# Products with v moved into the transposes' PSUM ring, with a new planner clock and new ranks

## The chip, the cores and the metric

The kernel runs on one core of one Trainium2 chip. What counts is device time in microseconds (us), from an execution's start to its end; with one core there is no slowest core to look for.

## What is computed

The reference runs three layers, one after another, in float32: attention that keeps only the 32 largest scores of each row, a dense layer with the gate h * cos(h), and a routed layer in which eight experts take 288 tokens each, handed out in the order of the logits.

```python
scores = scale * np.matmul(q, k.transpose(0, 1, 3, 2))          # 4 batches, 8 heads, 576 x 576, depth 64
kth = np.partition(scores, -top_k, axis=-1)[..., -top_k:-top_k + 1]
scores = np.where(scores >= kth, scores, -1000000000.0)
attn = np.exp(scores - np.max(scores, axis=-1, keepdims=True))
attn = attn / (np.sum(attn, axis=-1, keepdims=True) + 1e-09)
x = np.matmul(attn, v)                                          # then (2304, 512)
h = x @ w_in; y = (h * np.cos(h)) @ w_out                       # 512 -> 2048 -> 512
h = np.maximum(y[mask] @ w1[e], 0.0); out[mask] = h @ w2[e]     # per expert e, 288 tokens each
```

## The kernel before

**Stages.** The program has three stages. The first (phase1) runs attention and, behind it, the dense layer, interleaved. The second, the tail, finishes the dense layer and decides which token goes to which expert. The third runs the experts. The change touches the first stage and the ranks of the second.

**Attention in units.** Attention is cut into 72 units of 128 query rows with two "halves" h. The first eight (NWR) hold the 64 query rows left over from each head; the other 64 hold 128 rows of two heads each, and two units in a row share keys, queries and v (a pair, one `key`). Eight of these whole units feed one block of 256 tokens of the dense layer. One unit goes through these steps:

- qk (L555): PE (TensorE) writes half of the scores into the PSUM tile `two`, two banks; evac (L562): ACT (ScalarE) copies them into the tile x. This is done twice per unit, and both halves use the same columns of `two`, so the second qk follows the first evac.
- topk: DVE (VectorE) takes element-wise maxima and minima of the two halves (L596, L602) and then finds the 32 largest values by rounds of MAX8 and MATCH_REPLACE8 (L605, L609, L612); ACT, POOL (GpSimd) and DVE mask, exponentiate (L640) and clear (L645).
- tr (L710): PE transposes x into a PSUM tile of the ring pT, which has two tiles; eT (L720): ACT copies it out. Three such pieces belong to a whole unit.
- pv (L735, L737): PE multiplies eT with v. The result lies in `two` as well, in the columns behind the scores, one place per pair.
- The row sums become factors: div (L770, POOL), recip (L765, DVE), wide (L774, POOL), Rm (L781, PE, a transpose into the ring pT), Re (L784, ACT, into R), all once per pair; then scale (L798, DVE) multiplies pv's result of both units with R into xr. For the first eight units, scale is L795 and the factors are made per unit.

**The dense layer.** Each block's xr is split into a high and a low part xH, xL (L848, L853). mm1 (L287) makes hidden columns in pieces of 12 matmuls; sine and gate follow on ACT, DVE and POOL (`less` is L318 on DVE); mm2 (L887) multiplies back into the PSUM tiles pY in pieces of six. Of the eight banks of PSUM, `two`, pT, the hidden tiles pH and pY take two each.

**What sets the order.** A planner (class Plan) does. Each step is a task with an engine, a cost in ns, tasks it comes after, ring tiles it takes and gives back, and a rank: the unit or block number plus an offset per kind of task from the table OFFSETS (kinds of the first eight units end in _r, of the first block in _0). The planner simulates the engines, starts the earliest startable task of the lowest rank, and emits the instructions in that order; on the chip, each engine's queue runs strictly in it. For PE it adds a cost SW where the array's mode changes between tasks (scores 64x128, pv 128x64, the rest 128x128) and HOLD_PE to the rank of a task in another mode. The tail has a plan of its own, with TAIL_OFFSETS.

**Rings in pT.** Transposes of x, of the weights (wt), of y (yt), the small logit products and Rm take a tile of pT in the order of the plan, in turn; a tile is taken again when its reader has finished.

Of the kernel before, what the change touches and what calls it, by code (L numbers as in the profile page):

```python
# [14 lines left out]
AF = mybir.ActivationFunctionType  # L15
# [11 lines left out]
def f32(ap):  # L27
# [11 lines left out]
    "L": 4, "Re": 0.25, "Re_0": -5.25, "Re_r": 4.5, "Rm": 3.5, "Rm_0": -7.5, "Rm_r": -4.5, "bias": 7.25, "bias_0":  # L39
    2.75, "bias_r": -2, "big": -3, "big_0": -2.75, "big_r": -5.75, "count": -2, "div": 8, "div_0": 1.25, "div_r":  # L40
# [3 lines left out]
    -3.25, "large": 7.5, "large_0": 1, "large_r": 5.5, "less": 2.25, "less_0": 4.75, "low_in": -4.25, "low_out": 4,  # L44
# [3 lines left out]
    -5.5, "scale": -3.5, "scale_0": -1, "scale_r": -1.5, "sg_in": -10, "sg_out": 7, "shift_in": -9.75, "shift_out":  # L48
    -5.5, "sine": -4.5, "sine_0": 4, "small": 2.5, "small_0": -3.75, "small_r": -7.5, "strike": 3.75, "strike_0": 8,
    "strike_r": 6.25, "top": 7.25, "top_0": 7.25, "top_r": -3, "total": -8, "tr": -4, "tr_0": -10, "tr_r": -1.75,  # L50
    "v": 7.5, "wH_in": 6.25, "wH_out": -9.5, "wL_in": -3.25, "wL_out": -6.5, "w_in": 7, "w_out": 9.75, "whole": -5,
    "wide": -6, "wide_0": -5.25, "wl": 4, "wl_0": 3.25, "wp": 2.5, "wraw_in": 6.75, "wraw_out": -3.25, "wse": -1.75,
    "wst_out": -5.75, "wt": -9, "wte": -0.5, "xH": -5.75, "xL": -0.5, "yT": -10, "yd": -6.25, "ys": 4.75, "yt":
    0.75, "zero": 0.5, "zero_0": -5, "zero_r": -5.25
# [5 lines left out]
    "L": 3.75, "all": 0.75, "am": -3.5, "amd": -4.25, "any": -4.75, "asg": 0, "before": 0.75, "cmp": -4.75, "cnt":  # L60
    8.25, "columns": -9, "excess": -4, "first": 6.25, "gH": -6.75, "gH_e": -10, "gL": 5, "gL_e": -1.5, "gate": 1.25,
    "here": 1.75, "higher": -1.75, "hs": 1.75, "in_column": 0.5, "in_row": 1, "less": -8.5, "lg": -7, "lg4": 0.5,
    "listed": -1, "lt": 1.5, "mm1": 1.5, "mmT": 0.75, "near": -0.25, "next": -6.75, "numbers": 5.25, "places": 2.25,
    "prop": -3.75, "rise": -5.5, "rows": -3.5, "shares": 4, "sine": -3, "slots": -8, "square": -7.5, "start": 3.25,
    "sums": -5.5, "tokens": 0.25, "verdict": -2.5, "wh": 1.5, "wl": 6, "wlo": 7, "woL": 1, "woL_e": 0.75, "wrong":
    -10, "y": -1.5, "y_e": 3.25, "yd": 5, "yd_e": -0.5, "ys": -8, "ys_e": -6.75
# [3 lines left out]
class Plan:  # L70
# [6 lines left out]
    SW = 200  # L77
    HOLD_PE = 1.5
# [18 lines left out]

    def run(self):
        ts = self.tasks
        users, giver, left = {}, {}, {}  # L100
# [26 lines left out]
        while len(order) < len(ts):  # L127
# [54 lines left out]
def fused_kernel(ctx: ExitStack, tc: tile.TileContext, qT: bass.AP, kT: bass.AP, qR: bass.AP, kR: bass.AP, v9: bass.AP,  # L182
# [5 lines left out]
    HP = H // 2  # L188
# [54 lines left out]
    def everything(fold, ctx):  # L243
# [134 lines left out]
        def phase1():  # L378
# [13 lines left out]
            for vt in vts:  # L392
# [4 lines left out]
                pS=1, pPV=1, pT=2, pH=2, pY=1,  # L397
# [141 lines left out]
            def qk(j):  # L539
# [1089 lines left out]
```

## Time and profile before

| | |
|---|---|
| median of 3 runs | 1176.52 us (1175.04 to 1177.78) |
| profiled execution, its own time | 1176.04 us |
| its span, first to last instruction | 1174.1 us |
| PE busy | 1031.8 us (88%) |
| DVE busy | 903.1 us (77%) |
| ACT busy | 796.9 us (68%) |
| POOL busy | 515.2 us (44%) |
| mean granted clock of PE | 0.958 |

The profile is of one execution; 1.9 us of its time lie around the span. A row of the views below names engine, line and tiles: `PE two L555` is the scores' matmul of line 555 into the tile `two`. "A <- B" under waits means that A's engine stood idle until B was done. A busy time counts a matmul from its start to the end of its last result, so that matmuls in a row overlap: their steps are read from their starts.

### The profile page before, as it was taken

What the parts mean: (1) busy time and instruction counts of PE and PEld (TensorE: products, weight loads), DVE (VectorE), ACT (ScalarE), POOL (GpSimd) and SP (SyncE); (2) the same over time, 40 slices, a digit from 0 to 9 for tenths busy, and PEclk for the clock granted to TensorE, in tenths of its full rate; (3) what the DMA queues carried; (4) which work ended last, traced back from release to release, by engine and by line L of the source; (5) the groups of instructions that cost most, each with busy time, mean ns of one, the idle gap of its engine ahead of it and who ended that gap; (6) DMA issues with size and microseconds to landing.
All of it is one profiled execution on the core that took longest, in us unless ns stands there. A gap on an engine that the chain in (4) does not pass through costs nothing.

```text
span 1174.1 us, 22307 instructions
## 1 busy us (share of the span) xinstructions
PE 1031.8 (88%) x7952; PEld 861.6 (73%) x7952; DVE 903.1 (77%) x2443; ACT 796.9 (68%) x1431; POOL 515.2 (44%) x645
## 2 busy tenths in 40 slices
PE   4676898999899999999999999998898599999995
PEld 1344776777677777777777777777776499999995
DVE  6989999998898888888888888886469365555530
ACT  5876798888788787787887886888341255555531
POOL 5865676666554454454454553544200202222211
PEclk9876998999999999999999999999899899999998
DMA  7564353443323323223323223210043776666611
GB/s 228 164 184 150 108 158 113 129 148 115 104 89 98 94 78 100 85 82 97 92 81 103 80 82 102 79 55 6 34 160 128 228 211 201 185 187 198 185 40 43
DMA packets 86029, 141.08 MB, mean 120 GB/s; under 512 B 15248, under 2 KB 36240, under 8 KB 85904
## 3 DMA queue, kind: packets, MB, share of 16 engines
q1 hardware_dynamic: 82832, 130.07, 36.0%
q0 software_dynamic: 3072, 9.44, 2.7%
q8 instruction: 66, 1.08, 0.4%
q14 instruction: 59, 0.48, 0.1%
HBM read 125.85 MB, written 13.63 MB: 119 GB/s over the span
## 4 chain that ended last, share of the span: by engine, by line
PE 50%; issue 16%; ACT 14%; DVE 12%; POOL 5%; DMA 2%; SPq 0%; POOLq 0%; ACTq 0%; DVEq 0%
PE pH L287 13%; PE pY L887 11%; PE two L555 7%; PE two L737 4%; PE pT L710 4%; ACT x L562 4%; DVE w L609 2%; DVE m L605 2%; POOL out L1539 2%; PE pY L1403 2%; ACT eT L720 1%; PE ph L1507 1%; PE po L1522 1%; DVE cmp L1168 1%; PE two L735 1%
## 5 line engine op out<-in xcount | busy, mean ns | idle before, releaser
L605 DVE MAX8 m<-w 128x8 f32<-128x288 f32 (+1 forms) x576 | 238.1, 449 | 0.9
L555 PE MATMUL two<-kp,qp 64*128 64x288 f32 (+1 forms) x640 | 130.2, 496 | 77.6 <-ACT x L562 62.4
L609 DVE MATCH_REPLACE8 w<-m,w 128x288 f32<-128x288 f32 x432 | 188.8, 443 | 0.0
L287 PE MATMUL pH<-xH,wiH 128*128 128x256 f32 x576 | 173.7, 302 | 1.0 <-DVE kr L318 0.6
L287 PE MATMUL pH<-xL,wiH 128*128 128x256 f32 x576 | 163.8, 284 | 0.9 <-POOL xL L853 0.9
L287 PE MATMUL pH<-xH,wiL 128*128 128x256 f32 x576 | 163.4, 284 | 0.0
L562 ACT ACTIVATE x<-two 128x576 f32<-128x576 f32 x144 | 93.1, 646 | 71.6 <-PE two L735 56.3
L555 PEld LDWEIGHTS two<-kp,qp 64*128 64x128 f32 (+1 forms) x640 | 49.8, 189 | 123.6 <-ACT x L562 89.6
L720 ACT ACTIVATE eT<-pT 128x384 f32<-128x384 f32 x224 | 106.5, 480 | 23.1 <-PE pT L710 18.0
L633 POOL TENSOR_TENSOR x<-x,w 128x576 f32<-128x576 f32 x76 | 107.3, 1424 | 20.4 <-ACT w L627 20.2
L287 PEld LDWEIGHTS pH<-xH,wiH 128*128 128x128 f32 x576 | 110.3, 191 | 7.9 <-issue 5.6
L287 PEld LDWEIGHTS pH<-xL,wiH 128*128 128x128 f32 x576 | 110.8, 192 | 1.6 <-POOL xL L853 1.3
L287 PEld LDWEIGHTS pH<-xH,wiL 128*128 128x128 f32 x576 | 110.5, 192 | 0.0
L1023 DVE TENSOR_TENSOR w2l<-w2raw,w2h 128x1024 fp32r<-128x1024 f32 x64 | 77.9, 1223 | 41.8 <-ACT w2h L1020 41.8
L710 PE MATMUL pT<-ident,x 128*128 128x128 f32 x576 | 98.3, 280 | 2.2 <-ACT wog L830 1.5
L1539 POOL DMA_INDIRECT out<-ot,idx x24 | 22.3, 928 | 177.3 <-ACT ot L1537 176.9
L887 PE MATMUL pY<-wo,gH 128*128 128x512 f32 x224 | 95.5, 426 | 0.0
L710 PEld LDWEIGHTS pT<-ident,x 128*128 128x128 f32 x576 | 68.0, 141 | 31.7 <-issue 15.5
L328 POOL TENSOR_TENSOR hs<-hs,kr 128x512 f32<-128x512 f32 x56 | 73.1, 1312 | 40.6 <-ACT kr L323 34.2
L872 POOL TENSOR_TENSOR gL<-hs,gH 128x512 fp32r<-128x512 f32 x56 | 74.7, 1334 | 35.2 <-ACT gH L868 17.7
L887 PE MATMUL pY<-wl,gH 128*128 128x512 f32 x224 | 89.1, 398 | 0.0
L887 PE MATMUL pY<-wo,gL 128*128 128x512 f32 x224 | 88.2, 394 | 0.0
(220 smaller groups left out, 2874.8 us busy)
## 6 DMA issues: line engine op xcount, KB each, us to landing
w2raw<-w SPq DMA_DIRECT2D x64, 512.0 KB, 3.7
wl<-wl_d SPq DMA_DIRECT2D x112, 256.0 KB, 2.6
vt<-v SPq DMA_DIRECT2D x48, 256.0 KB, 2.7
kp<-kT SPq DMA_DIRECT2D x32, 288.0 KB, 3.2
room<-w_in SPq DMA_DIRECT2D x16, 512.0 KB, 5.0
room<-w_out SPq DMA_DIRECT2D x16, 512.0 KB, 3.5
woL<-wl_d SPq DMA_DIRECT2D x16, 512.0 KB, 3.6
kp<-kR SPq DMA_DIRECT2D x16, 288.0 KB, 4.3
```

Of the source, the lines that this page charges most:

```text
L287: PE.matmul(ph, lw[:, c, fs], rx[:, c, :], start=(k == 0), stop=(k == 3 * KD - 1))
L328: (G if m - 1 + i in GATE_POOL else V).tensor_tensor(h, h, T["kr", m // 2][:, 2 * i:2 * i + 2], op=OP.mult)
L555: PE.matmul(o, lhsT, T["kp", us[h]][p, s], start=True, stop=True)
L562: A.activation(T["x", j][:, :, c * hS:(c + 1) * hS], T["pS", (j, c)][:, :, :hS], AF.Copy)
L605: V.max(m8_(h, 8 * k), w_(h, 0, hS + (8 if k == TOPK // 8 - 1 else 0)) if fold else w_(h))
L609: V.match_replace(w, m8_(h, 8 * k), x_(h) if k == 0 and not fold else w, -BIG)
L633: G.tensor_tensor(x_(h), x_(h), w_(h), op=OP.subtract if mode == "S" else OP.add)
L710: PE.transpose(pT[:, i, :], e[:, c0:c0 + 128], ident)
L720: A.activation(new(ap, "eT", (j, c), [128, 3, 128])[:, :n], T["pT", ("e", j, c)][:, :n], AF.Copy)
L872: (G if m in GL_POOL else V).tensor_tensor(gL, T["hs", m], f32(T["gH", m]), op=OP.subtract)
L887: PE.matmul(T["pY", blk][t], T[g, m][:, i, ts], w, start=(f == 0 and n == 0), stop=(f == KF - 1 and n == 2))
L1023: eng.tensor_tensor(WS[n][1], WR.pop(n), f32(WS[n][0]), op=OP.subtract)
```

## The change

Three things change together.

**The products with v get a tile of the ring pT, one per unit.** pv takes a ring tile and no longer writes `two`. All that follows is done unit by unit instead of pair by pair: div, recip, wide, Rm, Re and scale run 64 times in place of 32 for the whole units, each on half the columns; the eight leftover units keep their count. pv now comes after Rm of its own unit, and the second piece of transposes of a unit comes after the pv of the unit before (the first piece, in the leftover units).

**The planner's costs.** The cost of a change of mode falls from 200 to 95 ns, HOLD_PE from 1.5 to 0; qk from 690 to 590 and pv from 1260 to 985. PE's work is now charged by a function that follows how busy the planned PE has been and counts its work at half speed while it takes the clock to be halved.

**The ranks** in OFFSETS and TAIL_OFFSETS are all replaced, so the order changes everywhere in the first stage, and a little in the second. Two lines of that table stand for it here.

```diff
-    "L": 4, "Re": 0.25, "Re_0": -5.25, "Re_r": 4.5, "Rm": 3.5, "Rm_0": -7.5, "Rm_r": -4.5, "bias": 7.25, "bias_0":
+    "L": -3.75, "Re": -2.25, "Re_0": -5.5, "Re_r": 6, "Rm": 4, "Rm_0": -2.25, "Rm_r": 5.5, "bias": 7, "bias_0":
...
-    SW = 200
-    HOLD_PE = 1.5
+    SW = 95
+    HOLD_PE = 0
...
+    def clock(self):
+        act, slow, since, W = 0.0, False, 0, self.WINDOW
+        def work(s, w):
...
+                speed = 0.5 if slow else 1.0
...
+        return work
...
+        work = self.clock()
...
-            f = s + t["ns"] + (self.TABLE if sw else 0)
             if t["mode"]:
-                f += self.SW if t["mode"] != mode else 0
+                f = work(s, t["ns"] + (self.SW if t["mode"] != mode else 0))
                 mode = t["mode"]
+            else:
+                f = s + t["ns"] + (self.TABLE if sw else 0)
...
-                pS=1, pPV=1, pT=2, pH=2, pY=1,
+                pS=1, pT=2, pH=2, pY=1,
...
                 def prod():
-                    if rem or t % 2 == 0:
-                        T["pPV", u] = two[:, :, hS:hS + 128]
-                    o_ = T["pPV", u]
+                    o_ = new(psum, "pT", ("pv", j), [128, 128])
...
-                    if c == 0 and ("Rm", key(j - 2, 0)) in plan.tasks and closes(j - 2):
-                        last.append(("Rm", key(j - 2, 0)))
+                    if j and c == (0 if rem else 1):
+                        last.append(("pv", j - 1))
...
-                add(("pv", j), "PE", 1700 if rem else 1260, prod, need + ([("pv", j - 1)] if j else []),
-                    [("pPV", u)] if rem or t % 2 == 0 else [],
+                add(("pv", j), "PE", 1700 if rem else 985, prod, need + [("Rm", j)] + ([("pv", j - 1)] if j else []), [("pT", "pv", j)],
                     need[:len(chunks)] + [("vt", w) for w in ((u, u + 1) if rem else (u, ))], rank=rank)
-                if not close:
-                    return
...
-                    G.tensor_scalar(ri[:, :, c], rs[:, :, c], TWO_PI, TWO_PI * 1e-9, op0=OP.mult, op1=OP.add)
+                    G.tensor_scalar(new(ap, "ri", j, [128, 2]), T["rs", j], TWO_PI, TWO_PI * 1e-9, op0=OP.mult, op1=OP.add)
...
-                        V.tensor_mul(xr[:, hp].rearrange("p (t q) -> p t q", t=2), pv_, R)
+                        V.tensor_mul(xr[:, hp, t % 2 * 128:(t % 2 + 1) * 128], o_, R[:, 0])
...
-                add(("scale", j), "DVE", 620 if rem else 345, scale, [("Re", u), ("pv", j)], [("xr", blk)] if firstw else [],
-                    [("R", u), ("pPV", u)], rank=rank)
+                add(("scale", j), "DVE", 620 if rem else 200, scale, [("Re", j), ("pv", j)], [("xr", blk)] if firstw else [],
+                    [("R", j), ("pT", "pv", j)], rank=rank)
```

Three places show how the order moves. Numbers behind a name tell buffers apart; line numbers of the change are its own (L589 is qk, L742 tr, L767 and L769 pv, L802 Rm, L325 mm1).

**Places 1 and 2, on PE, middle of the first stage.** Before: a unit's second qk, the products of an earlier unit, the next unit's first qk.

```order
L710 MATMUL pT_6689<-ident_64,x_6409 128x128 x3
L555 MATMUL two_119<-kp_6204,qp_6181 128x288 x2
L737 MATMUL two_119<-eT_6631,vt0_120 64x128 x3
L737 MATMUL two_119<-eT_6653,vt0_120 64x128 x3
L737 MATMUL two_119<-eT_6700,vt0_120 64x128 x2
L735 MATMUL two_119<-eT_6700,vt0_120 64x128 x2
L555 MATMUL two_119<-kp_6466,qp_6436 128x288 x2
L710 MATMUL pT_6732<-ident_64,x_6409 128x128 x3
```

The products stand between two qk there. Of the change, the same step, and as place 2 the two rows behind it:

```order
L589 MATMUL two_119<-kp_5955,qp_5896 128x288 x2
L769 MATMUL pT_6395<-eT_6319,vt0_120 64x128 x3
L769 MATMUL pT_6395<-eT_6347,vt0_120 64x128 x3
L769 MATMUL pT_6395<-eT_6382,vt0_120 64x128 x2
L767 MATMUL pT_6395<-eT_6382,vt0_120 64x128 x2
L589 MATMUL two_119<-kp_6171,qp_6146 128x288 x2
L742 MATMUL pT_6418<-ident_64,x_6121 128x128 x3
L802 MATMUL pT_6422<-ident_64,rw_6386 128x128
```

What stands side by side is the same, but the products write pT_6395, a ring tile, and not `two`. Behind them a piece of transposes takes the other tile of the ring, and Rm (pT_6422) the one that pT_6395 held; between the products and that Rm stand one qk and one tr.

On DVE, the scaling that gives such a tile back stood once per pair in the rounds of the top-k search, 128x256 long (xr is the scaled result, R the factors):

```order
L609 MATCH_REPLACE w_6439<-m8_6440,w_6439 128x288 x2
L605 MAX m8_6440<-w_6439 128x8 x2
L609 MATCH_REPLACE w_6439<-m8_6440,w_6439 128x288 x2
L605 MAX m8_6440<-w_6439 128x8 x2
L798 TENSOR_TENSOR xr_5782<-two_119,R_6565 128x256
L596 TENSOR_TENSOR w_6602<-x_6533 128x2x288
L645 SCALAR_TENSOR_TENSOR x_6409,rs_6548<-x_6409,m8_6440,w_6439 128x576
L602 TENSOR_TENSOR w_6602<-x_6533 128x2x288
```

It reads `two`, which qk writes. Now it stands there once per unit, 128x128:

```order
L643 MATCH_REPLACE w_6285<-m8_6286,w_6285 128x288
L639 MAX m8_6286<-w_6285 128x8 x2
L356 TENSOR_TENSOR kr_6202<-pH_6211,kr_6202 128x512
L643 MATCH_REPLACE w_6285<-m8_6286,w_6285 128x288 x2
L820 TENSOR_TENSOR xr_5901<-pT_6395,R_6349 128x128
L630 TENSOR_TENSOR w_6415<-x_6375 128x2x288
L639 MAX m8_6286<-w_6285 128x8
L636 TENSOR_TENSOR w_6415<-x_6375 128x2x288
```

It reads the ring tile pT_6395 of place 2, and stands ahead of the next unit's first top-k step (L630).

**Place 3, on PE, from the first stage to the tail.** Before, the last products were followed by the logit products L355, which read the table wog_, and only then by mm1 of the last block.

```order
L710 MATMUL pT_9547<-ident_64,x_9233 128x128 x3
L737 MATMUL two_119<-eT_9537,vt1_121 64x128 x3
L737 MATMUL two_119<-eT_9551,vt1_121 64x128 x3
L737 MATMUL two_119<-eT_9554,vt1_121 64x128 x2
L735 MATMUL two_119<-eT_9554,vt1_121 64x128 x2
L355 MATMUL pp_9647<-room_104,wog__9620 32x256 x16
L287 MATMUL pH_9678<-xH_101,wiH_99 128x256
L287 MATMUL pH_9678<-xL_102,wiH_99 128x256
L287 MATMUL pH_9678<-xH_101,wiL_100 128x256
```

Behind L355 stood all of that mm1. In the change:

```order
L742 MATMUL pT_9935<-ident_64,x_9629 128x128 x3
L802 MATMUL pT_9940<-ident_64,rw_9912 128x128
L769 MATMUL pT_9947<-eT_9930,vt1_121 64x128 x3
L769 MATMUL pT_9947<-eT_9933,vt1_121 64x128 x3
L769 MATMUL pT_9947<-eT_9942,vt1_121 64x128 x2
L767 MATMUL pT_9947<-eT_9942,vt1_121 64x128 x2
L325 MATMUL pH_10039<-xH_101,wiH_99 128x256
L325 MATMUL pH_10039<-xL_102,wiH_99 128x256
L325 MATMUL pH_10039<-xH_101,wiL_100 128x256
```

Now mm1 of the last block follows at once; four pieces of it, 48 matmuls, stand ahead of the logit products (L393 in the change).

## Rows read from the trace of the kernel before

**Rows 1.** Busy us (xinstructions) of PE, PEld, DVE, ACT, POOL; granted clock, DMA share, GB/s
```profile
0.00:118.90 118.90, 73.54 (x572) 40.87 (x572) 100.15 (x291) 79.60 (x155) 79.22 (x84) 0.81 0.59 182
118.90:226.70 107.80, 94.86 (x702) 77.09 (x701) 100.57 (x270) 91.89 (x173) 75.60 (x84) 0.92 0.41 127
226.70:818.10 591.40, 547.34 (x4276) 446.26 (x4275) 515.31 (x1531) 478.64 (x860) 296.73 (x388) 1.00 0.30 89
```

**Rows 2.** The same view for one period of the long stretch
```profile
572.68:659.13 86.45, 79.76 (x618) 64.78 (x617) 74.80 (x225) 68.77 (x123) 42.16 (x57) 1.00 0.30 89
```

**Rows 3.** Waits of PE, 226.7 to 818.1: us in total, times, longest us
```profile
PE two L555 <- ACT x L562: 39.0, 51, 0.8
```

**Rows 4.** Timeline of PE: start us, us, line, out<-in, [idle before <-releaser]
```profile
514.08 0.76 PE L555 MATMUL two<-kp,qp 64*128 64x288 f32 x4
514.76 1.09 PE L737 MATMUL two<-eT,vt 128*64 128x128 f32 x16
515.69 0.39 PE L735 MATMUL two<-eT,vt 128*64 128x128 f32 x4
516.85 0.76 PE L555 MATMUL two<-kp,qp 64*128 64x288 f32 x4 [0.78 <-ACT x L562]
```

**Rows 5.** Timeline of ACT, same place
```profile
516.15 0.65 ACT L562 ACTIVATE x<-two 128x576 f32<-128x576 f32 x1 [1.61 <-PE two L735]
```

**Rows 6.** Waits of DVE, 226.7 to 818.1
```profile
DVE w L596 <- ACT x L562: 24.8, 17, 4.0
DVE xr L798 <- PE two L555: 22.8, 12, 3.4
```

**Rows 7.** Timeline of PE, hidden matmuls and the scores behind them
```profile
500.65 0.28 PE L287 MATMUL pH<-xL,wiH 128*128 128x256 f32 x1
500.77 0.28 PE L287 MATMUL pH<-xH,wiL 128*128 128x256 f32 x1
500.99 0.76 PE L555 MATMUL two<-kp,qp 64*128 64x288 f32 x4
```

**Rows 8.** Groups of 226.7 to 818.1: shapes xcount | busy us, mean ns | idle before
```profile
L798 DVE TENSOR_TENSOR xr<-two,R 128x256 f32<-128x256 f32 x27 | 11.3, 420 | 23.4 <-PE two L555 22.8 <-ACT R L784 0.3
L765 DVE RECIPROCAL ri<-ri 128x4 f32<-128x4 f32 x28 | 4.5, 162 | 0.3 <-POOL ri L770 0.3
L770 POOL TENSOR_SCALAR ri<-rs 128x4 f32<-128x4 f32 x28 | 10.3, 369 | 78.7 <-DVE x L645 73.3 <-DVE fa L964 4.7
L774 POOL COPY rw<-ri 128x256 f32<-128x256 f32 x28 | 11.6, 416 | 10.0 <-DVE ri L765 10.0
```

**Rows 9.** Groups of 0 to 118.9, DVE
```profile
L795 DVE TENSOR_TENSOR xr<-two,R 64x128 f32<-64x128 f32 x14 | 4.0, 288 | 2.8 <-PE two L555 2.4
```

**Rows 10.** Waits of DVE, 0 to 118.9
```profile
DVE room L435 <- ACT room L428: 8.8, 2, 6.1
DVE w L596 <- ACT x L562: 2.6, 2, 2.3
DVE xr L795 <- PE two L555: 2.4, 1, 2.4
```

**Rows 11.** Waits of DVE, 118.9 to 226.7
```profile
DVE xr L798 <- PE two L555: 3.1, 3, 1.6
DVE xr L795 <- PE two L555: 1.7, 1, 1.7
```

**Rows 12.** Waits of PE, 0 to 118.9
```profile
PE two L555 <- DVE xr L795: 5.8, 3, 3.3
```

**Rows 13.** Timeline of PE, end of the attention phase
```profile
817.67 0.44 PE L735 MATMUL two<-eT,vt 128*64 128x128 f32 x4
826.50 3.64 PE L355 MATMUL pp<-room,wog__9620 128*32 128x256 f32 x32 [8.40 <-DVE wog__9620 L1077]
```

**Rows 14.** Timeline of DVE, same place
```profile
820.39 0.42 DVE L853 TENSOR_TENSOR xL<-xr,xH 128x256 fp32r<-128x256 f32 x1
825.58 0.56 DVE L1077 COPY wog__9620<-wog 128x128 f32<-128x128 f32 x1
```

More of the change, by code (lines that the diff above doesn't have):

```diff
@@ L50 @@
[L50 to L54, printed above, removed]
+    "L": -3.75, "Re": -2.25, "Re_0": -5.5, "Re_r": 6, "Rm": 4, "Rm_0": -2.25, "Rm_r": 5.5, "bias": 7, "bias_0":
@@ L59 @@
 TAIL_OFFSETS = {
[L60 to L66, printed above, removed]
+    "L": 5.25, "all": -6.25, "am": -7.5, "amd": 5, "any": -0.5, "asg": 6.75, "before": -5, "cmp": -8, "cnt": -1.75,
+    "columns": 2.75, "excess": -5.75, "first": 1.5, "gH": 1.5, "gH_e": 1, "gL": 5, "gL_e": 0.5, "gate": -3.5,
+    "here": 1.5, "higher": 2.25, "hs": -3.25, "in_column": -1.75, "in_row": 4, "less": 3.25, "lg": -4.75, "lg4":
+    -1.5, "listed": -7, "lt": -1.25, "mm1": -2.25, "mmT": 4.25, "near": 5, "next": 2.5, "numbers": 7.75, "places":
+    2, "prop": -7, "rise": -0.75, "rows": 6.25, "shares": -0.75, "sine": 0.25, "slots": -6, "square": -1.5, "start":
+    -5.5, "sums": 6, "tokens": -0.5, "verdict": 3.5, "wh": -7, "wl": -7.75, "wlo": -4.75, "woL": -8.5, "woL_e": -6,
+    "wrong": -7, "y": 0.75, "y_e": 1.75, "yd": 3.75, "yd_e": 1.25, "ys": 0.75, "ys_e": 4.75
 }
@@ L783, in spread_out @@
+                    for n in range(2 if rem else 1):
+                        PE.transpose(p[:, n], T["ri", j][:, n:n + 1].to_broadcast([128, 128]) if rem else
+                                     T["rw", j].rearrange("p h d -> p (h d)"), ident)
                 def spread_out():
-                    A.activation(new(ap, "R", u, [128, 2, 128]), T["pT", ("R", u)], AF.Copy)
+                    A.activation(new(ap, "R", j, [128, 2, 128])[:, :2 if rem else 1], T["pT", ("R", j)], AF.Copy)
                 blk = 0 if rem else 1 + (j - NWR) // (2 * HP)
@@ L808, in pv @@
-                firstw = j == 0 if rem else (j - NWR) % (2 * HP) == 1
-                add(("scale", j), "DVE", 620 if rem else 345, scale, [("Re", u), ("pv", j)], [("xr", blk)] if firstw else [],
-                    [("R", u), ("pPV", u)], rank=rank)
+                        V.tensor_mul(xr[:, hp, t % 2 * 128:(t % 2 + 1) * 128], o_, R[:, 0])
+                exps = [("zero" if MODES[j] == "T" else "exp", a) for a in range(2 * j, 2 * j + 2)]
+                add(("div", j), "POOL", 190, div, exps, [("ri", j)], [("rs", j)], rank=rank)
@@ new lines, in pv @@
+                add(("recip", j), "DVE", 85, recip, [("div", j)], rank=rank)
+                if not rem:
+                    add(("wide", j), "POOL", 300, wide, [("recip", j)], [("rw", j)], [("ri", j)], rank=rank)
+                add(("Rm", j), "PE", 220 if rem else 110, spread, [("recip" if rem else "wide", j)], [("pT", "R", j)],
+                    [("ri" if rem else "rw", j)], rank=rank)
+                add(("Re", j), "ACT", 265 if rem else 165, spread_out, [("Rm", j)], [("R", j)], [("pT", "R", j)], rank=rank)
@@ L856, in block @@
                 for c in range(HP):
-                    need = [("scale", w) for w in last if unit(w)[2] // 2 == c // 2] if blk == 0 else [("scale", last[c])]
+                    need = [("scale", w) for w in last if unit(w)[2] // 2 == c // 2] if blk == 0 else [("scale", last[2 * c + i]) for i in range(2)]
                     add(("xH", blk, c), *(("DVE", 340) if (blk, c) == LAST else ("ACT", 310)), x_high(c), need + ([("xH", blk, c - 1)] if c else []),
```

91 lines of the change are left out of this document (54 added, 37 removed), and 9 rows, old and new, of the table OFFSETS.

## Prediction, written before the changed kernel was run

> **What bounds the kernel now.** I read the table of stretches first, since the share of busy time over the whole span mixes four stages. Up to 226.7 us VectorE (DVE) is the fuller engine: 100.15 of 118.9 us, then 100.57 of 107.8, against 73.54 and 94.86 for TensorE (PE) [rows 1]. From 226.7 to 818.1 us PE takes over: 547.34 of 591.4 us at a granted clock of 1.00 (the 2.4 GHz level), DVE 515.31. In that stretch the work repeats: eight units of attention and eight hidden pieces every 86.45 us, with PE busy 79.76 and DVE 74.80 [rows 2]. A microsecond that PE saves there is a microsecond of the kernel, as long as DVE can follow.
>
> Next the waits. PE's 44 us of idleness in the stretch are nearly one item: 51 times scores (L555) waited for the evacuation of the scores before (ScalarE, ACT, L562), 39.0 us, at most 0.8 each [rows 3]. The timeline shows why. Scores start at 514.08; the products with v (L737, L735) follow and end at 515.69 + 0.39 = 516.08; the next scores start at 516.85, after 0.78 us of waiting [rows 4]. The evacuation of the first scores, ready to run at 514.84, starts at 516.15, just after the last product [rows 5]: scores and products lie in the same two PSUM banks, and the read is held until PE has stopped writing there. The same sharing hits DVE: its scaling of the products (L798) waited 22.8 us for PE's scores, and its first top-k step (L596) 24.8 us for the evacuation [rows 6].
>
> **The change part by part.** *Products out of `two`.* The evacuation (0.65 us) now runs beside the products, which take 514.76 to 516.08 = 1.32 us: it is done before PE has finished them, so the 39.0 us go. Place 1 shows scores, products, scores still side by side; they need not move.
>
> *More changes of array mode.* Scores, products and the rest each have a mode of the array. By the order, PE changes mode 32 times per eight units before, 36 after. Hidden matmuls start 0.12 us apart (500.65, 500.77), the scores behind them 0.22 after the last [rows 7]: a change costs 0.10 us. The stretch is 591.4 / 86.45 = 6.8 periods, so 4 x 6.8 = 27 more, +2.7 us. The Trainium skill (TensorEngine Tiling (Array Packing), Key Properties) says that a change of tiling mode drains TensorE, which speaks against the new order; were a whole matmul's 0.28 us exposed at each change, not the step's 0.12, a change would be an estimated 0.16 and the sum 1.6 us later. The row shows less, and I stay with it.
>
> PE's floor of the stretch: 591.4 - 39.0 + 2.7 = **555.1 us**.
>
> *Scaling per unit on DVE.* 27 scalings of 128x256 at 420 ns become 54 of 128x128 [rows 8]. No row has that shape: half of 420 is the lower end (0 more in all), 420 unchanged the upper (+11.3). I take 288, that of the 64x128 scaling [rows 9], nearest in columns: 54 x 0.288 - 27 x 0.420 = +4.2. The reciprocals double, 28 x 0.162 = +4.5. DVE work: 524.0 us. DVE is idle for 591.4 - 515.3 = 76.1 us; without the 22.8 (the false wait for scores) and the 24.8 there are 28.5 left. So DVE's path is 524.0 + 28.5 = 552.5 us if the waits for the evacuation vanish, 577.3 if all stay, 564.9 with half. Each evacuation comes up to 1.3 us earlier, 17 x 1.3 = 22 of the 24.8; but only where nothing else is late.
>
> Floor (555.1) and DVE (552.5 to 564.9) thus lie on top of each other, and two full engines in step lose a little to each other. I take the middle of 555.1 and 564.9, **560.0: -31.4 us**. Ends: 577.3 (-14.1), and 547.3 + 2.7 = 550.0 if PE's other waits vanish too (-41.4).
>
> *Cost at nothing.* POOL gets 28 more divisors and 28 more widenings, 28 x (0.369 + 0.416) = 22.0 us [rows 8], on 296.7 busy in 560: hidden behind PE and DVE. ACT gets 27 copies of R, at most an evacuation's 0.65 each, 17.6 on 478.6: 496 of 560, hidden; were ACT the bound, those 17.6 would be the price. PE transposes as many R columns as before.
>
> *The new wait.* The products now need R's transposes first, so divisor, reciprocal and widening (0.369 + 0.162 + 0.416 = 0.95 us and three hand-overs) stand ahead of them. Place 2 has that transpose behind the first three transposes of x; queued behind it on PE are mm2 and the next products, and ACT and DVE wait for those. This is why I take the middle, not the floor.
>
> *The start (0 to 226.7).* DVE sets it. False waits of the same kind are 2.6 + 2.4 [rows 10] and 3.1 + 1.7 us [rows 11], 9.8 together; five pairs add 5 x (0.576 - 0.420 + 0.162) = 1.6. Half of 9.8 less 1.6: **-3.3**. The ranks are new here, so ends far apart: all DVE idleness but the 8.8 for the first weights gone, 26.0 - 8.8 - 1.6 = -15.6; or +5.8, if PE's wait for scalings there (5.8) [rows 12] comes back at the ring.
>
> *The hand-over.* After the last products, at 817.67 + 0.44 = 818.11, PE waits until 826.50 for a table that DVE finishes at 825.58 + 0.56 = 826.14 [rows 13, 14]. Place 3: 48 hidden matmuls (48 x 0.12 = 5.8 us) now come first; they need xL, ready at 820.39 + 0.42 = 820.81. They fill 826.50 - 820.81 = **-5.7**; other end 0, if the last hidden pieces aren't what the routing waits for. Behind it the rows of the order stay the same.
>
> Sum: -31.4 - 3.3 - 5.7 = -40.4 on the profiled execution's 1176.04: 1135.6. Its time is 0.48 under the median of the runs, so I forecast **1136 us**. Ends: -41.4 - 15.6 - 5.7 = -62.7 (1114) and -14.1 + 5.8 + 0 = -8.3 (1168).
>
> **The rivals.**
>
> *The ring stalls (slower).* A product holds one of two ring tiles until DVE has scaled it; in place 2 the second request behind it (R's transpose) comes 0.68 (scores) + 3 x 0.12 = 1.04 us after the products. If DVE is behind by the mean of today's waits between the two, 22.8 / 12 = 1.9 us, PE waits 1.9 + 0.29 - 1.04 = 1.15 us in each of 64 units, 73 us: **1209**. It decides from 40.4 / 64 = 0.63 us per unit. For it: in the start, where DVE is the bound, PE did wait for scalings [rows 12]. Against it: in the long stretch DVE waits for PE, not PE for DVE. 0.07.
>
> *The wait only changes its name (no change).* If scaling waits for the products as long as it did for scores and the evacuation's 24.8 stay, DVE's path is 577.3 + 22.8 = 600.1, +8.7: 1176.5 + 8.7 - 3.3 - 5.7 = **1176**. For it: each scaling does follow its product on another engine, and now twice as often. Against it: it waited for scores that were issued later than its data. 0.05.
>
> *The banks aren't parted.* Were PSUM still shared, PE would keep its 39.0: 1176.5 + 2.7 - 5.7 = **1173.5**. Against it: the ring's tiles are separate allocations, and transposes there do not hold up evacuations today. 0.03.
>
> *The clock falls.* In the second stretch PE idled for 12.9 of 107.8 us and was granted 0.92, a mix of its two levels, 1.2 and 2.4 GHz [rows 1]. At 0.92 the long stretch would be 550.0 / 0.92 = 597.8, +6.4: **1174**. Against it: its 51 short waits went by at 1.00, and there will be fewer. 0.04. The Trainium skill (TensorE: Matmul & The Clock Gate, A second HAM failure mode: psum-queue depth-cycling) has a kernel whose cycling through PSUM made the clock swing by small pauses, as a ring of two with five users a unit might; the trace, at 1.00 through 51 pauses, does not bear it out.
>
> **How the numbers follow.** The forecast has 0.81. Its own range is 1114 to 1168, of which I trust 0.95: 0.77. Up to 1174 the clock and the unparted banks come in: 0.84. A measurement of this kernel tells 0.2% (2.4 us) from no change: faster 0.85 (the forecast and half of those two), same 0.06, slower 0.09 (the ring, and part of the renamed wait).
>
> **What would show it.** Right: scores no longer wait for evacuations behind products; the period is near 82 us (86.45 x 560.0 / 591.4) with PE over 97% busy; the phase ends near 783 us, and the hidden matmuls follow without 8 us of idleness. Wrong: PE waits at transposes or R's transposes for scalings or widenings over 0.2 us per unit, DVE waits at scaling of 20 us or more, or a clock below 1.00 in the middle.

## The result, and the profile after

The changed kernel takes **1120.42 us** (median of 4 runs, 1118.34 to 1123.02) against 1176.24 (4 runs of the kernel before, taken beside it): a ratio of 0.953, with a 95% interval of 0.950 to 0.955, or 55.8 us less. The forecast was 1136 us in 1114 to 1168, and up to 1174 with two of the rivals counted in.

The page of the changed kernel, busy time by engine (its span is 1118.4 us, 1174.1 before):

```profile
PE 1026.4 (92%) x7952; PEld 859.9 (77%) x7952; DVE 914.7 (82%) x2507; ACT 799.0 (71%) x1463; POOL 542.1 (48%) x709
```

PE does the same work in less time. To see where, both traces have to be cut where the same work is done, not at the same microsecond. I cut at the end of the products of the ninth whole unit (unit 17, with the eight leftover units ahead of it), at the end of the last products, and at the experts' first transposes (934.48 and 877.87 us). Behind the first cut both kernels still have 1284 hidden matmuls (mm1) and 612 of mm2 to do in the attention phase. The table of stretches (columns as in [rows 1]) of the kernel before, cut so:

```profile
0.00:237.30 237.30, 178.82 (x1362) 127.06 (x1362) 211.29 (x591) 181.02 (x348) 161.33 (x174) 0.87 0.50 155
237.30:818.10 580.80, 536.92 (x4188) 437.17 (x4186) 504.74 (x1502) 469.11 (x841) 290.21 (x382) 1.00 0.30 88
818.10:934.50 116.40, 89.43 (x680) 72.06 (x679) 69.81 (x182) 32.15 (x51) 16.30 (x23) 0.91 0.40 133
934.50:1174.10 239.60, 226.62 (x1728) 225.28 (x1728) 117.27 (x170) 114.64 (x194) 47.40 (x68) 0.96 0.51 156
```

The same of the changed kernel, with one period of eight units (551.80 to 631.10) as the third row:

```profile
0.00:234.40 234.40, 179.06 (x1368) 126.62 (x1368) 216.59 (x594) 180.70 (x353) 164.32 (x185) 0.88 0.51 158
234.40:770.80 536.40, 533.03 (x4180) 437.29 (x4180) 509.80 (x1563) 471.03 (x866) 312.99 (x435) 1.00 0.31 95
551.80:631.10 79.30, 79.30 (x618) 65.01 (x618) 75.89 (x233) 68.73 (x127) 46.16 (x64) 1.00 0.32 97
770.80:877.90 107.10, 87.17 (x681) 70.33 (x679) 71.02 (x182) 32.65 (x52) 15.09 (x22) 0.96 0.42 142
877.90:1118.40 240.50, 227.10 (x1728) 225.71 (x1728) 117.25 (x170) 114.58 (x194) 49.70 (x69) 0.96 0.51 157
```

So the start gains 2.9 us, the long stretch 580.8 - 536.4 = **44.4**, the way from the last products to the experts 9.3, and the experts lose 0.9: together 55.7, the whole difference of the spans. In the long stretch PE is busy 533.0 of 536.4 us. A period takes 79.30 us, not 86.45 [rows 2], and PE has no idle time in it.

The waits of the changed kernel, PE's and then DVE's, 234.4 to 710.5 us (us in total, times, longest us):

```profile
PE two L589 <- ACT x L596: 1.0, 2, 0.7
PE pT L841 <- DVE xr L820: 0.6, 1, 0.6
PE pT L802 <- POOL rw L797: 0.3, 1, 0.3
PE pT L742 <- ACT eT L752: 0.3, 1, 0.3
```

```profile
DVE xr L820 <- PE pT L767: 5.9, 17, 0.7
DVE w L630 <- POOL x L667: 3.5, 6, 0.6
DVE ri L791 <- POOL ri L794: 3.4, 4, 0.9
...
DVE w L630 <- ACT x L596: 0.2, 1, 0.2
```

PE's 39.0 us of waiting for evacuations [rows 3] have become 1.0, also when the window runs to 770.8 us. Of DVE's two false waits [rows 6], 24.8 and 22.8 us, what is left is 0.2 for the evacuation and 5.9 for the products themselves (7.3 up to 770.8 us). At the ring of two, PE waited for a scaling once: transposes of weights (L841), 0.6 us.

Why the evacuation no longer holds PE shows in two timelines (start us, us). First PE, then ACT:

```profile
746.94 0.76 PE L589 MATMUL two<-kp,qp 64*128 64x288 f32 x4
747.62 1.09 PE L769 MATMUL pT<-eT,vt 128*64 128x128 f32 x16
748.55 0.39 PE L767 MATMUL pT<-eT,vt 128*64 128x128 f32 x4
748.87 0.55 PE L742 MATMUL pT<-ident,x 128*128 128x128 f32 x3
```

```profile
747.74 0.65 ACT L596 ACTIVATE x<-two 128x576 f32<-128x576 f32 x1 [0.30 <-PE two L589]
```

The evacuation starts 0.12 us after the products do and runs beside them. Before, it started after the last product [rows 4, 5]. The profile infers from the semaphores what released the evacuation: the scores (L589) in the changed kernel, the last product (L735) in the kernel before [rows 5]. By that it was held by the program's own synchronisation, for columns that it doesn't read. Scores and products were parts of one tile, `two`, and so of the same banks; no run has them as two tiles in one bank, so it stays open whether the tile or the bank makes the wait. The next PE work starts 748.87 - 747.62 = 1.25 us after the first product.

The groups that the change added, 234.4 to 770.8 us (columns as in [rows 8]):

```profile
L820 DVE TENSOR_TENSOR xr<-pT,R 128x128 f32<-128x128 f32 x55 | 15.7, 285 | 8.0 <-PE pT L767 7.3
L791 DVE RECIPROCAL ri<-ri 128x2 f32<-128x2 f32 x55 | 8.4, 153 | 4.1 <-POOL ri L794 3.7
L806 ACT ACTIVATE R<-pT 128x128 f32<-128x128 f32 x55 | 15.2, 276 | 0.1
```

### The profile page after: what moved, and what is told of

Its sections match the earlier page's. It is cut to its first block, busy times and chain, and to the rows that moved or that the text cites. A ratio compares the mean times of both kernels' runs of the same rounds, so it can differ in the third digit from the quotient of the medians.

```text
span 1118.4 us, 22436 instructions
## 1 busy us (share of the span) xinstructions
PE 1026.4 (92%) x7952; PEld 859.9 (77%) x7952; DVE 914.7 (82%) x2507; ACT 799.0 (71%) x1463; POOL 542.1 (48%) x709
## 5 line engine op out<-in xcount | busy, mean ns | idle before, releaser
L325 PE MATMUL pH<-xH,wiH 128*128 128x256 f32 x576 | 173.3, 301 | 0.5 <-DVE xr L820 0.5
L325 PE MATMUL pH<-xL,wiH 128*128 128x256 f32 x576 | 162.7, 282 | 0.0
L325 PE MATMUL pH<-xH,wiL 128*128 128x256 f32 x576 | 162.5, 282 | 0.0
L589 PE MATMUL two<-kp,qp 64*128 64x288 f32 (+1 forms) x640 | 130.7, 498 | 26.3 <-ACT x L596 18.4
L325 PEld LDWEIGHTS pH<-xH,wiH 128*128 128x128 f32 x576 | 109.9, 191 | 5.4 <-issue 4.0
L325 PEld LDWEIGHTS pH<-xL,wiH 128*128 128x128 f32 x576 | 109.9, 191 | 0.3
L325 PEld LDWEIGHTS pH<-xH,wiL 128*128 128x128 f32 x576 | 109.7, 190 | 0.0
L1561 POOL DMA_INDIRECT out<-ot,idx x24 | 22.3, 927 | 175.2 <-ACT ot L1559 174.7
L742 PE MATMUL pT<-ident,x 128*128 128x128 f32 x576 | 98.0, 279 | 3.9 <-DVE x L678 1.6
L589 PEld LDWEIGHTS two<-kp,qp 64*128 64x128 f32 (+1 forms) x640 | 50.2, 190 | 66.6 <-ACT x L596 28.7
L366 POOL TENSOR_TENSOR hs<-hs,kr 128x512 f32<-128x512 f32 x56 | 75.8, 1371 | 42.7 <-ACT kr L361 42.0
L742 PEld LDWEIGHTS pT<-ident,x 128*128 128x128 f32 x576 | 67.8, 142 | 31.2 <-issue 14.0
L894 POOL TENSOR_TENSOR gL<-hs,gH 128x512 fp32r<-128x512 f32 x56 | 75.7, 1352 | 30.8 <-ACT gH L890 24.7
```

The costliest lines, as they stand in the source:

```text
L325: PE.matmul(ph, lw[:, c, fs], rx[:, c, :], start=(k == 0), stop=(k == 3 * KD - 1))
L366: (G if m - 1 + i in GATE_POOL else V).tensor_tensor(h, h, T["kr", m // 2][:, 2 * i:2 * i + 2], op=OP.mult)
L589: PE.matmul(o, lhsT, T["kp", us[h]][p, s], start=True, stop=True)
L742: PE.transpose(pT[:, i, :], e[:, c0:c0 + 128], ident)
L894: (G if m in GL_POOL else V).tensor_tensor(gL, T["hs", m], f32(T["gH", m]), op=OP.subtract)
```

## The experiments

The change has three parts that can be taken apart: where the products lie (the banks), the planner's costs, and the ranks. **Theory A**, the prediction's, says that the parted banks give the gain. The rival, **theory B**, says that the new order gives it. Ratios are to the kernel before, with 95% intervals.

### Products back into the scores' banks

```diff
-                    o_ = new(psum, "pT", ("pv", j), [128, 128])
...
+                    o_ = two[:, :, hS:hS + 64] if rem else two[:, t % 2, hS:hS + 128]
+                    T["pT", ("pv", j)] = o_
```

Plan and order stay those of the change.

> The changed kernel with its order and all its tasks as they are, but the products with v written into the banks of the scores again. Theory A (the parted banks give the gain): the evacuation waits for the products behind scores again, 30 places with scores, products, scores in a row cost PE some 0.8 us each, 24 us, and DVE waits at the scaling or the first top-k step again; 1142 to 1168 us. Theory B (the new order and ranks give it): within 5 us of the changed kernel, 1116 to 1126.

Measured: 1173.3 us, ratio 0.996 (0.994 to 0.998). Its waits, 234.6 to 748 us, PE and DVE:

```profile
PE two L589 <- ACT x L596: 22.3, 29, 0.8
PE two L589 <- DVE xr L819: 1.9, 3, 0.7
```

```profile
DVE xr L819 <- PE two L589: 28.9, 24, 1.9
DVE w L630 <- ACT x L596: 4.7, 4, 1.5
DVE xr L819 <- ACT x L596: 4.7, 7, 0.9
```

B falls: with all of the new order, but shared banks, the old waits are back and the gain is gone. The time lies 5 us above A's range. Of the 53.0 us between the two spans, 34.1 arise in units 9 to 56 (PE idles for 26.7 us there, against 3.0) and 15.7 before them. A had 24 in all; why the start is longer was not taken apart.

### Old ranks with parted banks

```diff
-    "L": -3.75, "Re": -2.25, "Re_0": -5.5, "Re_r": 6, "Rm": 4, "Rm_0": -2.25, "Rm_r": 5.5, "bias": 7, "bias_0":
+    "L": 4, "Re": 0.25, "Re_0": -5.25, "Re_r": 4.5, "Rm": 3.5, "Rm_0": -7.5, "Rm_r": -4.5, "bias": 7.25, "bias_0":
...
```

All of OFFSETS and TAIL_OFFSETS are those of the kernel before.

> The changed kernel with both tables of ranks of the kernel before; banks parted, new planner costs. Theory A: most of the gain stays, 1120 to 1145 us, PE over 95% busy in the middle. Theory B: most of it goes, 1155 us or more, with PE waiting at transposes and factors for the ring.

Measured: 1175.52 us, ratio 1.000 (0.998 to 1.002). A falls too, as far as it says that parting the banks is enough. B has the time, but not its reason, as units 9 to 56 show, first of the kernel before, then of this one (the second row of each has the waits: us in total, times, longest us):

```profile
217.20:742.40 525.20, 484.39 (x3748) 393.34 (x3746) 461.88 (x1375) 422.66 (x758) 268.58 (x348) 1.00 0.32 97
PE two L555 <- ACT x L562: 35.9, 47, 0.8
```

```profile
237.90:745.00 507.10, 494.90 (x3779) 400.41 (x3779) 461.39 (x1380) 423.27 (x775) 281.12 (x389) 1.00 0.33 97
PE two L589 <- ACT x L596: 3.5, 6, 1.3
```

With the old ranks, too, the parted banks take away the wait for evacuations, 35.9 us against 3.5, and PE idles only 12.2 us. The 48 units gain 18.1 us, although 72 hidden matmuls more are done beside them (36 of mm1, 36 of mm2). The start loses 20.7, and nothing is left. The old ranks were found for the old planner costs, though, and this run has the new ones; the parted banks with old ranks and old costs were not run.

### Shared banks, new planner and new ranks

This is the kernel before with the Plan class, the two tables of ranks and the costs of qk and pv of the change.

```diff
-    "L": 4, "Re": 0.25, "Re_0": -5.25, "Re_r": 4.5, "Rm": 3.5, "Rm_0": -7.5, "Rm_r": -4.5, "bias": 7.25, "bias_0":
+    "L": -3.75, "Re": -2.25, "Re_0": -5.5, "Re_r": 6, "Rm": 4, "Rm_0": -2.25, "Rm_r": 5.5, "bias": 7, "bias_0":
...
-    SW = 200
-    HOLD_PE = 1.5
+    SW = 95
+    HOLD_PE = 0
...
```

> The kernel before (products in the banks of the scores, scaled pair by pair) with the new planner, its costs and both new tables of ranks. Theory A: 1155 us or more, with 0.8 us per scores, products, scores in a row (23 places by the order) and waits of DVE for scores. Theory B: under 1140.

Measured: 1168.33 us, ratio 0.992 (0.990 to 0.995). PE waited 21.7 us for evacuations and DVE 22.1 between 232 and 748 us. The new order does not remove these waits. What it does gain here is no more than the tail's ranks give by themselves (below).

### The change with the older planner

```diff
-    SW = 95
-    HOLD_PE = 0
+    SW = 200
+    HOLD_PE = 1.5
...
-                speed = 0.5 if slow else 1.0
+                speed = 1.0
```

> The changed kernel with the old price of a mode change (200 ns), the old hold (1.5) and no halved clock in the planner. Theory A: 1116 to 1135 us, PE still nearly full in the middle. Theory B: the order it gives was not what the ranks were found for, 1140 or more.

Measured: 1144.45 us, ratio 0.974 (0.971 to 0.976), so as B had it: banks and ranks of the change, planned with other costs, give less than three fifths of the gain. (The costs of qk and pv are still those of the change.)

### The tail's ranks alone

This is the kernel before with TAIL_OFFSETS of the change, and nothing else.

```diff
-    "L": 3.75, "all": 0.75, "am": -3.5, "amd": -4.25, "any": -4.75, "asg": 0, "before": 0.75, "cmp": -4.75, "cnt":
+    "L": 5.25, "all": -6.25, "am": -7.5, "amd": 5, "any": -0.5, "asg": 6.75, "before": -5, "cmp": -8, "cnt": -1.75,
...
```

> The kernel before, with only the tail's ranks of the change; banks, planner and the first stage's ranks stay as they were. Theory A (the 9.3 us that the change gains between the last products and the first transposes of the experts come from the hidden matmuls moved ahead of the logit products, and need nothing of the rest): 1165 to 1170, 6 to 9 us under the kernel before, and PE's idleness behind the last products falls from 8.4 us to under 3. Theory B (the tail is shorter because the first stage leaves less work behind): 1174 to 1178, no difference.

Measured: 1168.11 us, ratio 0.994 (0.992 to 0.996), 8.7 us less: A. The stretches behind the last products, first of the kernel before, then of this one:

```profile
818.10:826.50 8.40, 0.00 (x1) 0.03 (x1) 6.58 (x23) 3.10 (x6) 5.82 (x14) 0.72 0.34 126
826.50:835.00 8.50, 8.50 (x66) 6.47 (x67) 0.00 (x0) 1.79 (x4) 3.33 (x3) 0.67 0.00 0
```

```profile
819.00:827.00 8.00, 6.08 (x48) 5.86 (x48) 6.60 (x23) 4.97 (x10) 5.46 (x14) 1.00 0.38 132
827.00:835.00 8.00, 7.24 (x72) 6.61 (x76) 4.50 (x7) 3.99 (x7) 3.79 (x4) 1.00 0.01 2
```

Before, PE idled for 8.4 us and then ran at a granted clock of 0.67, a mix of its two levels. The same 32 logit matmuls took 3.64 us there [rows 13], and here, at 1.00, as below. In the changed kernel they took 2.93, behind a wait of 2.27 us.

```profile
833.70 1.93 PE L355 MATMUL pp<-room,wog__9620 128*32 128x256 f32 x32
```

### Only the planned clock taken out

```diff
-                speed = 0.5 if slow else 1.0
+                speed = 1.0
```

> The change, except that the planner counts PE at full speed throughout; the smaller cost of a mode change and the rank bonus of 0 stay, and so do banks and ranks. Theory A (the planned clock matters in the first 235 us alone, where the chip's clock is below 1.00; the rest of the loss of the older planner came from mode change cost and rank bonus): 1121 to 1132, with the middle's period within 1 us of 79.3. Theory B (the ranks fit one planner only, and any change of a cost breaks the order): 1140 or more, with PE waits in the middle too.

Measured: 1138.99 us, ratio 0.970 (0.965 to 0.975). Both theories miss something. The start is as fast as in the change (unit 17 ends at 233.9 us), but the middle isn't: 497.6 us from the end of the eighth whole unit to that of the 56th, against 479.3. PE hardly waits there, as this row (217.8 to 715.4 us) shows against that of the change (218.9 to 698.2) below it:

```profile
217.80:715.40 497.60, 491.68 (x3780) 400.11 (x3778) 465.93 (x1406) 423.97 (x782) 287.82 (x396) 1.00 0.34 102
```

```profile
218.90:698.20 479.30, 476.31 (x3726) 390.39 (x3724) 462.30 (x1411) 417.42 (x772) 283.94 (x390) 1.00 0.33 102
```

PE is as full as in the change, but does more in that stretch: 491.7 us of work, 54 matmuls more. So the order must have pulled work of a later time forward.

### Only the ranks of the start taken back

The ranks of the first eight units and of the first hidden block (names in _r and _0) are those of the kernel before. Four of the 52 entries that differ stand for all.

```diff
-    "Re_0": -5.5, "Re_r": 6, "Rm_0": -2.25, "Rm_r": 5.5,
+    "Re_0": -5.25, "Re_r": 4.5, "Rm_0": -7.5, "Rm_r": -4.5,
...
```

> The change, with the ranks of the kernel before for the first eight units and the first hidden block alone; the ranks of the steady units and of the tail are those of the change. With all ranks old, the products of unit 17 ended 25.0 us later than in the change, the middle took 27.1 us more to unit 57, and the last six units and the tail about 6. Theory A (start and middle lose separately): 1135 to 1150, unit 17 ends 12 us or more later, and the middle's period stays within 1 us of 79.3. Theory B (the loss is in the steady ranks, the start only follows them): 1119 to 1126.

Measured: 1154.92 us, ratio 0.983 (0.980 to 0.986). Both fall. Unit 17 ends at 230.2 us, 4 earlier than in the change, and yet the middle is slow (510.0 us for the same 48 units), with the steady ranks untouched.

These misses led to a **third theory**. I counted, from the timeline of PE, the mm2 matmuls issued by the end of the products of whole unit 56 (from here on whole units are counted 1 to 64): 600 in the change, 636 without the planned clock, 660 with the old start ranks, 672 with all ranks old. All have 672 by unit 64. Work left for the last eight units seemed to cost nothing, and work done before to cost PE time in the middle, where PE is full.

### One rank, to move 72 matmuls, and 60

```diff
-    "mm2": 9.25
+    "mm2": 7
```

> The change, with one rank altered: that of the steady mm2 pieces, 7 instead of 9.25. In its order all 672 mm2 matmuls of the attention phase stand ahead of the products of unit 56, where the change has 600 and leaves 72 for the last eight units. In every version so far the last eight units took 72.6 to 77.7 us, whether 72, 54, 36, 12 or 0 mm2 stood beside them; one mm2 takes 0.247 us of PE. Theory A (attention alone bounds the last eight units, so what hidden work is left for them is free, and what is done earlier costs PE time in the middle, where PE is full): 72 x 0.247 = 17.8 us slower, 1134 to 1144, with the last eight units at 72 us or more. Theory B (PE bounds the last units too, the work only changes place): 1119 to 1124, with the last eight units near 55 us.

Measured: 1144.11 us, ratio 0.972 (0.971 to 0.974). With a rank of 10:

```diff
-    "mm2": 9.25
+    "mm2": 10
```

> The same with a rank of 10, so on the other side of the change's 9.25: in the order 660 mm2 stand ahead of the products of unit 56, 60 more than in the change. Theory A: 60 x 0.247 = 14.8 us slower, 1131 to 1141. Theory B: 1119 to 1124.

Measured: 1142.84 us, ratio 0.972 (0.970 to 0.974). Both lie just past the upper ends of A's ranges, and 19 to 20 us above B's. The last eight units, of the change and of the kernel with rank 7:

```profile
698.20:770.80 72.60, 71.68 (x584) 60.29 (x582) 62.93 (x193) 66.58 (x122) 40.95 (x59) 1.00 0.18 56
```

```profile
732.00:801.10 69.10, 57.50 (x494) 47.69 (x494) 59.66 (x186) 56.99 (x104) 26.40 (x46) 0.90 0.09 25
```

With 90 matmuls fewer beside them (12 of mm1 went ahead with the 72) the last units gain 3.5 us, not 18; PE idles instead, and its clock falls to 0.90. At 69.1 us they lie under the 72 that A named, and far above B's 55. (The range of 72.6 to 77.7 us in the expectation leaves out the older planner's 80.7.) From unit 8 to unit 56 the kernel with rank 7 takes 511.6 us, 32.3 more than the change. Its row says that 501.42 - 476.31 = 25.1 of these are PE work and 10.2 - 3.0 = 7.2 idleness:

```profile
220.40:732.00 511.60, 501.42 (x3813) 405.47 (x3812) 471.12 (x1418) 430.59 (x791) 296.45 (x403) 1.00 0.34 100
```

So the theory holds in kind, and priced at 17.8 us it was too cheap: the altered order also waits more, and its PE work grows by more than the 72 mm2. By the distances from one start to the next, waits included, 22.4 of the 32.3 us lie on mm2 and 8.8 on the transposes of x. Nor was the work at the end free: without it the last units take 3.5 us less, and what follows them 6.3 less (the logit products don't wait there; in the change they wait 2.27 us).

### Only the steady ranks taken back

Five of the 63 entries that differ stand for all.

```diff
-    "L": -3.75, "Re": -2.25, "Rm": 4, "bias": 7, "big": 5.75
+    "L": 4, "Re": 0.25, "Rm": 3.5, "bias": 7.25, "big": -3
...
```

> The change, with the steady units' ranks of the kernel before; the ranks of the first eight units, of the first hidden block and of the tail are those of the change. In the order 666 mm2 stand ahead of the products of unit 56, 66 more than in the change. Theory A (as above): at least 66 x 0.247 = 16.3 us slower, 1136 to 1160, most of it between units 8 and 56. Theory B (the start is what matters): 1119 to 1126.

Measured: 1159.25 us, ratio 0.985 (0.983 to 0.988): A.

### Scaling twice

```diff
-                        V.tensor_mul(xr[:, hp, t % 2 * 128:(t % 2 + 1) * 128], o_, R[:, 0])
+                        for _ in range(2):
+                            V.tensor_mul(xr[:, hp, t % 2 * 128:(t % 2 + 1) * 128], o_, R[:, 0])
```

> The change, with the scaling of each of the 64 whole units executed twice, in the same order: 64 x 0.285 = 18.2 us more work on DVE, of which 55 x 0.285 = 15.7 in the long stretch. DVE was busy 509.8 of 536.4 us there. Theory A (DVE lies within 5% of PE, so that what is added eats its 26.6 us of idleness and then shows): half or more of the work shows, 1128 to 1138, and PE waits for scalings or evacuations reappear. Theory B (PE alone bounds the stretch, and DVE's slack takes the work): 1120 to 1124.

Measured: 1131.64 us, ratio 0.961 (0.958 to 0.964), 11.2 us over the change for 18.2 us of work: A. In the profiled execution, the slowest of the four, the long stretch takes 545.1 us, 8.7 more for 15.7 of added work; PE waits for scalings are back with 3.8 us. The start takes 6.5 more, which the 2.6 us of scalings added there don't explain. DVE is nearly a second bound.

### All of them by stretch

Ends of the products read from the timelines of PE; "rest" is from the end of unit 64 to the end of the span.

| kernel | median us | unit 8 ends | units 9 to 56 | mm2 by unit 56 | units 57 to 64 | rest |
|---|---|---|---|---|---|---|
| before | 1176 | 217.2 | 525.2 | 618 | 75.7 | 356.0 |
| the change | 1120 | 218.9 | 479.3 | 600 | 72.6 | 347.6 |
| shared banks | 1173 | 234.6 | 513.4 | 600 | 74.5 | 348.9 |
| old ranks | 1176 | 237.9 | 507.1 | 672 | 74.0 | 357.3 |
| shared banks, new order | 1168 | 232.0 | 516.4 | 642 | 75.0 | 344.3 |
| older planner | 1144 | 221.7 | 491.3 | 600 | 80.7 | 344.3 |
| tail's ranks alone | 1168 | 218.2 | 525.1 | 618 | 75.7 | 348.5 |
| no planned clock | 1139 | 217.8 | 497.6 | 636 | 77.7 | 345.7 |
| old start ranks | 1155 | 220.7 | 510.0 | 660 | 77.1 | 344.4 |
| old steady ranks | 1159 | 218.3 | 515.6 | 666 | 77.8 | 346.8 |
| mm2 at 7 | 1144 | 220.4 | 511.6 | 672 | 69.1 | 341.3 |
| mm2 at 10 | 1143 | 216.5 | 504.0 | 660 | 74.4 | 344.8 |
| scaling twice | 1132 | 225.7 | 485.5 | 600 | 74.8 | 347.5 |

Three things can be read from it. The rest is 7 us or more longer with the old tail ranks (356.0 and 357.3 against 341.3 to 348.9). The last eight units take 69 to 81 us whatever is beside them. And units 9 to 56 take less than 500 us only with parted banks, and there only where 600 or 636 mm2 stand ahead of the end of unit 56; with 660 to 672 they take 504 to 516. Parting the banks is worth 34.1 us of that stretch in the new order (513.4 to 479.3), and 18.1 with the old ranks.

## Why the prediction was right, and where its sizes were off

**What bounds the kernel: right.** In the long stretch PE was the bound and the 39.0 us of false waits were what it had to give. With the banks shared again, and everything else kept, 22.3 us of them are back (29 waits).

**The long stretch: right mechanism, sized too small.** The step that failed reads "I take the middle of 555.1 and 564.9, 560.0: -31.4 us"; measured is -44.4, past the end of -41.4. Three pieces make the 13.0 us between them: 2.8, 5.3 and 4.9.

- *The price of one wait.* I took 0.78 us each, the idle time that the trace states. That time is counted from the modelled end of the products, 1.32 us after their start; the changed kernel shows that other work can start after 1.25. Taking the time from each row's start to the next row's start in PE's timeline, products followed by scores cost 1.165 us for their last four matmuls before (50 times) and 0.330 after (33 times). So one wait cost 0.835, and 50 of them 41.8, 2.8 over my 39.0. The products as a whole took 110.7 us of the stretch before and 69.2 after; scores (70.7 and 70.6) and hidden matmuls (315.1 and 316.8) hardly changed.
- *PE's other waits, and the mode changes.* All idleness fell from 580.80 - 536.92 = 43.9 us to 3.4; I had left 5 us of it in place. By the same distances the transposes of x and the waits around them took 55.1 us before and 51.9 after, 3.2 less. The mode changes show as the 1.7 more on hidden matmuls, 1.0 under the 2.7 that I added. The last 1.1 of the 5.3 I can't assign to one kind.
- *DVE's share.* I added 4.9 us because two full engines lose to each other: a term that no row had priced. In this order they lost nothing that shows. DVE was idle for 26.6 of 536.4 us, where the lowest of my three paths left it 28.5. Still, the scaling done twice shows how little room there is.

**More changes of mode: right in number and price.** The timeline of the stretch has 213 before and 238 after, 25 more where I had 27. A step from a hidden matmul to scores takes 0.21 us against 0.126 between hidden matmuls, so about 0.09 each where I had 0.10; there are 39 such steps, 19 before. The Trainium skill (TensorEngine Tiling (Array Packing), Key Properties) speaks of a drain at each change; the trace has the 0.09 and no more.

**Scaling per unit: right.** 288 ns taken, 285 measured; 162 taken for the reciprocal, 153 measured. DVE's work in the stretch grew by 5.1 us (504.7 to 509.8), where I had 8.7.

**Cost at nothing, and the new wait: right.** Up to 710.5 us PE waited 0.5 us for widenings, 0.3 of it at R's transposes, and 0.6 for a scaling. POOL's added work is on its busy time (290.2 to 313.0), not on the path.

**The start: right in sign, and in size partly by luck.** -3.3 taken and -2.9 measured, by another cut. DVE's waits at scalings and for evacuations fell by 5.8 us (9.8 to 4.0), where I had half of 9.8, and its other idleness by 2.4; its work grew by 5.3 (211.3 to 216.6), where I had 1.6. The misses cancel. Cut one unit earlier the changed kernel is 1.7 us behind (218.9 against 217.2), with 30 matmuls more done.

**The hand-over: right mechanism, sized too small.** -5.7 taken; -9.3 measured, and -8.7 with the tail's ranks alone. The term counted the idleness behind the last products and not the slow clock after it: behind 8.4 us without work the logit matmuls took 3.64 us, and the first hidden ones 0.21 us each instead of 0.12. The tail's ranks alone, with the clock at 1.00, bring the logit matmuls to 1.93. The change recovers part of that (2.93): of its 9.3 us, 7.0 are less idleness of PE and 2.3 less busy time for the same work.

**"They need not move": the step that was too easy.** The prediction credited the parted banks with the gain and treated the ranks as nearly neutral, looking at three places of the order. The runs show that parted banks with the old ranks and the new planner costs gain nothing in all, and that the new order with shared banks gains no more than its tail does. The wait for evacuations comes and goes with the shared banks, with old ranks and new; whether the time that it frees is kept depends on the order. What the ranks do isn't visible at the places I quoted. Among other things they set how much mm2 is left for the last eight units, and moving that by one rank cost 22 to 24 us. Nothing of this was priced in the prediction: with parted banks and one set of ranks or costs or another, the runs lie between 1120 and 1176 us. That this order was the one that keeps the gain is luck as far as the forecast goes.

**The rivals.** The ring did not stall; the waits did not change their name (7.3 us left of 47.6); the clock stayed at 1.00 in the long stretch. What the Trainium skill (TensorE: Matmul & The Clock Gate, A second HAM failure mode: psum-queue depth-cycling) tells of a kernel whose clock swung by cycling through PSUM did not come about here: the granted clock was 1.00 over the 536.4 us.

**What stays open.** What the parted banks give with the old ranks and the old planner costs was not run. I can't say what bounds the last eight units: PE at 57.5 and DVE at 59.7 of 69.1 us are both short of full in the kernel with rank 7. Nor is it shown which single ranks beside that of mm2 matter. With the older planner 600 mm2 stand ahead of unit 56, as in the change, and still the middle takes 12.0 us more and the last units 8.1 more; so the count of mm2 is not all of it. This is order, too, but I did not find which part.

## What to carry to other kernels

Two results that share a PSUM tile and its banks can make an engine wait for data that it doesn't read: look in the timeline for a reader that starts only when PE has finished something else, and price the wait by the distance between starts, not by the idle time alone. When an order comes from a planner, a resource that is freed and the order that uses it are one change: test each alone before crediting either. And count what hidden work is left for a phase's end, where the bound engine has room: work that was pulled forward into a full stretch cost its full time here, and more.

## What the runs showed of the hardware

- A long idle gap of PE cost more than its length. Behind 8.4 us without work the granted clock was 0.67 for the next 8.5 us, a mix of 1.2 and 2.4 GHz; in the run with the tail's ranks alone, with 1.50 us without work at that place, it stayed at 1.00. In the changed kernel PE waits 2.27 us ahead of its logit products at 779.57 us, and the 8 us around and behind them are at 0.79 (in the long stretch before, 51 waits of up to 0.8 us went by at 1.00):

```profile
779.00:787.00 8.00, 7.43 (x65) 6.04 (x66) 4.17 (x6) 2.33 (x5) 4.14 (x4) 0.79 0.01 2
```

- The same instruction's mean moves with the order. DVE's first top-k step on 128x576 took 869 ns on average before and 790 after in the long stretch, while the masking step took 820 and then 886 (first two rows before, last two after):

```profile
L596 DVE TENSOR_TENSOR w<-x 128x576 f32<-128x576 f32 x53 | 46.0, 869 | 29.5 <-ACT x L562 24.8 <-POOL x L633 4.3
L645 DVE SCALAR_TENSOR_TENSOR x<-x,m,w 128x576 f32<-128x576 f32 x54 | 42.9, 820 | 1.9 <-ACT w L640 1.8
L630 DVE TENSOR_TENSOR w<-x 128x576 f32<-128x576 f32 x53 | 41.9, 790 | 5.1 <-POOL x L667 3.5 <-POOL gL L894 1.1 <-ACT x L596 0.2
L678 DVE SCALAR_TENSOR_TENSOR x<-x,m,w 128x576 f32<-128x576 f32 x54 | 47.0, 886 | 2.1 <-ACT w L673 2.0
```

The two cancel here, 4.1 us each. What causes it was not tried.
